# Two unused strips in SBUF that move every operand of the two MLPs

## Chip, cores and metric

The kernel runs on one core of a Trainium2 chip. The metric is the device time of one execution in microseconds (us). Before the change it is 952.58 us, the median of three runs (951.78 to 953.23).

## What is computed

The reference is a linear attention over 4 x 8 heads of 576 x 64, whose output, laid out as 2304 tokens of 512 features, goes through two MLPs one after the other:

```
phi(x): proj = x @ w_phi; proj -= max|proj|; concat(exp(proj), exp(-proj))
attn = (phi(q) @ (phi(k)^T v)) / (phi(q) . sum(phi(k)) + 1e-6)
MLP 1: h = x @ w_in;  g = h if h > 0 else exp(min(h, 0)) - 1;   x = g @ w_out
MLP 2: h = x @ w_in;  g = h * clip(h + 3, 0, 6) / 6;            y = g @ w_out
```

Both MLPs have 512 features and 2048 hidden units. Their weights arrive as 64-bit floats and are turned into 32-bit floats on the chip.

## The kernel before

**Order of work.** A planner (`in_order`) gives every step an engine, a length and a rank and writes out one order for all engines; TensorE's order in the MLPs is written by hand (the list `order`). Attention takes the first 158 us or so, in eight units; the rest is the MLPs.

**How an MLP is tiled.** The tokens are cut into four blocks of 512 and one of 256 (`BLOCKS`). The hidden units are walked in 8 groups g of 256 per MLP (g = 0 to 7 is MLP 1, g = 8 to 15 is MLP 2). For the blocks in pairs (pr = 0 and pr = 1) the first product is made in Strassen's way, from seven products P1 to P7 whose token operands are the tiles A11, A12, A22, S1, S2, S3 and S4 of that pair; the last block goes the plain way (`hid4`). The tables that say which operand a product uses are:

```
TERMS = {
    "P1": ("A11", "B11"), "P2": ("A12", "B21"), "P3": ("S4", "B22"), "P4": ("A22", "T4"),
    "P5": ("S1", "T1"), "P6": ("S2", "T2"), "P7": ("S3", "T3"),
}
```

**The matmuls.** Every 32-bit operand is kept as a high and a low part in the type fp32r, and a product is three matmuls: high x high, high x low, low x high. There are three kinds of matmul group:
- P groups (`hid`, L710): six matmuls of 512 columns; the weights `w_in` are stationary, the token tile `x_...` moves. 14 in each g.
- H groups (`hid4`, L724): twelve matmuls of 256 columns with the token tile `x_b4`. 2 in each g.
- O groups (`outp`, L775): six matmuls. In MLP 1 the stationary operand is `w_out` and the gated tile `ga` or `gb` moves, 512 columns for 16 groups of each g and 256 columns for 4; in MLP 2 `ga`/`gb` is stationary and `w_out` moves, always 512 columns, 18 groups in each g.

In a middle g the order is: H, O, H, O O O, P1 P2 of pair 0, O O, P6, O O, P5 P7, P1 of pair 1, P3 of pair 0, O, P4 of pair 0, O, P2 of pair 1, O O, P6, O O, P5 P7, O, P3, O, P4, O O (from P2 on all of pair 1; the two O after P3 and P4 of pair 0 are the last block's). The profile drops buffer numbers: `x_A` is any of A11, A12, A22 and `x_S` any of S1 to S4, so this order says which one a row is.

**What is done around them.** ScalarE and VectorE gate a finished P or H group in PSUM (L744 to L758: the last two write the high and low parts of `ga`/`gb`), VectorE adds finished O groups to the sum in `x32` (L787), ScalarE, VectorE and GpSimd convert and split weights (L626 to L677). A P or H group needs a free PSUM bank, which the low part (L758) of an earlier group frees. Between the MLPs, at g = 8, the token operands are made anew from the finished sums (`prepare`, L687 to L696).

**Where the tiles lie.** SBUF is filled from both ends of each partition, and each tile begins on a multiple of 32 bytes. From the left: 1,152 bytes of scratch and constants, then `x32` at 1,152, `ident` at 38,016, `half_c` and `two_c`, and the unused tile `gap` (496 bytes) at 38,592. After it come the pools `wp` (`w_in`, `w_out`), `stg` (the conversion), `early` (five operands of pair 0: A11, A12, A22, S1, S3) and `att_b`, later `mlp_b` (all seven operands of pair 1). `wp` begins at 39,104 = 76 x 512 + 192, all its tiles and those of the other MLP pools are whole multiples of 512 bytes long, and the slices that TensorE reads begin at multiples of 512 within a tile: so these operands all begin at remainder 192, counted modulo 512. From the right: the pools of attention and later `mlp_a` (S2 and S4 of pair 0, `x_b4`, `ma`, `mb`, `ga`, `gb`), which ends at 229,344 = 447 x 512 + 480: these all begin at remainder 480.

Of the kernel before, what the change touches and what calls it, by code (L numbers as in the profile page):

```python
# [8 lines left out]
F32 = mybir.dt.float32  # L9
# [139 lines left out]
def attention_then_two_mlps(  # L149
# [49 lines left out]
    const = ctx.enter_context(tc.tile_pool(name="const", bufs=1))  # L199
# [17 lines left out]
    nc.gpsimd.memset(half_c, 0.5)  # L217
    two_c = const.tile([128, 1], F32, name="two_c")
    nc.gpsimd.memset(two_c, 2.0)
    const.tile([128, 124], F32, name="gap")  # L220

    wp = ctx.enter_context(tc.tile_pool(name="wp", bufs=1))
    stg = ctx.enter_context(tc.tile_pool(name="stg", bufs=1))
# [928 lines left out]
```

## Time and profile before

| | |
|---|---|
| median of three runs | 952.58 us |
| the profiled execution | 952.91 us |
| its span, first to last instruction | 950.8 us |
| TensorE matmul busy | 918.8 us (97% of the span) |
| TensorE weight load busy | 762.3 us (80%) |
| VectorE, ScalarE, GpSimd busy | 676.0, 566.6, 399.7 us |
| mean granted TensorE clock | 0.990 |

Busy times of TensorE are of pipelined instructions: each matmul of 512 columns is shown some 390 to 397 ns long, and the next one starts long before it ends. The pace is therefore read from the starts: in a timeline of TensorE alone, a row is a run of equal matmuls, and the start of the next row less its own start, over its count, is the time of one. Its starts are rounded to 0.01 us.

### The profile page before, as it was taken

The page shows a single profiled execution, that of the slowest core. Times are in us where ns is not written, and L with a number is a line of the kernel's source. Part 1 is how long each engine was busy: PE and PEld are TensorE (multiplying, and loading weights), DVE is VectorE, ACT ScalarE, POOL GpSimd, SP SyncE. Part 2 cuts the span into 40 slices and gives each one's busy share as a digit, 9 for nine tenths or more (in the row PEclk, how much of TensorE's full clock was granted, in tenths as well). Part 3 has the DMA queues.
Part 4 walks back from the last instruction along what each step waited for, and adds up shares of the span by engine and source line. Part 5 has one row for each costly group of instructions (what it writes and reads, how often), then busy time and mean ns, then how long its engine had stood idle before and what let it go on. Part 6 is the DMA issues. An engine that isn't in the chain of part 4 may idle for free.

```text
span 950.8 us, 17635 instructions
## 1 busy us (share of the span) xinstructions
PE 918.8 (97%) x6792; PEld 762.3 (80%) x6792; DVE 676.0 (71%) x1202; ACT 566.6 (60%) x1207; POOL 399.7 (42%) x570
## 2 busy tenths in 40 slices
PE   8999999899999999999999968999999999999998
PEld 7888787688888888888878856888888888888886
DVE  6888877855676767676767797467767676777555
ACT  5686766876665656565666755665545454545331
POOL 0258621453544444444442646545444444444200
PEclk9999999999999999999999987999999999999999
DMA  8534510001111111111111001111111111010013
GB/s 228 160 110 124 147 47 2 1 27 41 45 45 45 45 46 45 45 44 46 45 42 43 29 22 36 43 56 55 46 56 34 57 34 56 33 56 23 1 67 133
DMA packets 42532, 53.69 MB, mean 56 GB/s; under 512 B 21328, under 2 KB 21456, under 8 KB 42448
## 3 DMA queue, kind: packets, MB, share of 16 engines
q1 hardware_dynamic: 42448, 52.57, 17.8%
q8 instruction: 53, 0.87, 0.4%
q14 instruction: 31, 0.25, 0.1%
HBM read 47.84 MB, written 4.72 MB: 55 GB/s over the span
## 4 chain that ended last, share of the span: by engine, by line
PE 88%; DVE 6%; ACT 5%; issue 1%; POOL 0%; POOLq 0%; ACTq 0%
PE ps_a L775 27%; PE ps_p L710 25%; PE ps_t L775 13%; PE ps_t L710 6%; PE ps_t L430 4%; PE ps_a L380 4%; PE ps_p L724 3%; PE ps_p L318 3%; ACT e L407 2%; DVE x L687 1%; DVE x_S L696 1%; PE ps_t L452 1%; PE ps_t L724 1%; DVE x L787 1%; DVE x_A L696 1%
## 5 line engine op out<-in xcount | busy, mean ns | idle before, releaser
L710 PE MATMUL ps_p<-x_S,w_in 128*128 128x512 f32 x630 | 162.6, 397 | 10.0 <-POOL x_S L696 4.1
L787 DVE TENSOR_TENSOR x<-ps_a,x 128x512 f32<-128x512 f32 (+1 forms) x177 | 116.4, 660 | 50.4 <-PE ps_a L775 49.0
L710 PEld LDWEIGHTS ps_p<-x_S,w_in 128*128 128x128 f32 x630 | 118.4, 189 | 39.4 <-POOL x_S L696 4.9
L710 PE MATMUL ps_p<-x_A,w_in 128*128 128x512 f32 x468 | 120.9, 399 | 3.4 <-DVE ga L758 3.4
L668 POOL TENSOR_TENSOR w_in<-w_bi,w_in 128x256 fp32r<-128x256 f32 x128 | 97.7, 782 | 44.7 <-ACT w_in L664 44.2
L635 POOL TENSOR_SCALAR w_a<-w_a 128x256 f32<-128x256 f32 x128 | 53.9, 422 | 146.5 <-ACT w_a L630 146.1
L710 PEld LDWEIGHTS ps_p<-x_A,w_in 128*128 128x128 f32 x468 | 88.5, 191 | 23.3 <-DVE ga L758 4.2
L787 DVE TENSOR_TENSOR x<-ps_t,x 128x512 f32<-128x512 f32 (+1 forms) x89 | 59.0, 663 | 43.0 <-PE ps_t L775 42.6
L651 POOL TENSOR_TENSOR w_bi<-w_bi,w_a 128x256 int32<-128x256 int32 x64 | 47.9, 757 | 95.0 <-DVE w_a L647 95.0
L677 POOL TENSOR_TENSOR w_out<-w_bo,w_out 128x256 fp32r<-128x256 f32 x64 | 48.1, 751 | 94.3 <-ACT w_out L673 93.6
L775 PE MATMUL ps_a<-w_out,gb 128*128 128x512 f32 x336 | 84.9, 395 | 0.0
L775 PE MATMUL ps_a<-gb,w_out 128*128 128x512 f32 (+1 forms) x384 | 83.2, 358 | 0.6 <-DVE x L787 0.6
L651 POOL TENSOR_TENSOR w_bo<-w_bo,w_a 128x256 int32<-128x256 int32 x64 | 48.3, 756 | 65.0 <-DVE w_a L647 62.3
L775 PEld LDWEIGHTS ps_a<-gb,w_out 128*128 128x128 f32 x384 | 64.8, 188 | 13.2 <-DVE x L787 0.8
L775 PEld LDWEIGHTS ps_a<-w_out,gb 128*128 128x128 f32 x336 | 63.0, 188 | 15.1 <-ACT x L785 0.2
L751 DVE SCALAR_TENSOR_TENSOR ps_p<-ma,ps_p 128x512 f32<-128x512 f32 x66 | 45.8, 693 | 30.8 <-ACT ma L747 16.4
L775 PE MATMUL ps_a<-ga,w_out 128*128 128x512 f32 x258 | 65.6, 395 | 0.5 <-DVE ga L758 0.5
L732 ACT COPY mb<-ps_p 128x512 f32<-128x512 f32 x54 | 31.7, 587 | 57.1 <-PE ps_p L710 56.9
L328 DVE TENSOR_REDUCE mx<-ps_p 128x4 f32<-128x512 f32 (+1 forms) x80 | 50.3, 629 | 15.7 <-PE ps_p L318 15.4
L775 PE MATMUL ps_a<-w_out,ga 128*128 128x512 f32 x240 | 60.1, 397 | 0.0
L775 PEld LDWEIGHTS ps_a<-ga,w_out 128*128 128x128 f32 x258 | 47.6, 188 | 11.6 <-DVE ga L758 0.9
L630 ACT ACTIVATE w_a<-w 128x256 f32<-128x256 f32 x128 | 54.3, 424 | 1.1 <-POOL w_bo L651 1.1
(109 smaller groups left out, 1907.1 us busy)
## 6 DMA issues: line engine op xcount, KB each, us to landing
w<-in_moe_w_in_dram SPq DMA_DIRECT2D x64, 256.0 KB, 2.6
w<-in_moe_w_out_dram SPq DMA_DIRECT2D x64, 256.0 KB, 2.6
vb<-in_v_dram SPq DMA_DIRECT2D x16, 288.0 KB, 4.2
out_dram<-x SPq DMA_DIRECT2D x18, 256.0 KB, 2.0
raw_k<-in_k_dram SPq DMA_DIRECT2D x7, 576.0 KB, 4.5
raw_q<-in_q_dram SPq DMA_DIRECT2D x7, 576.0 KB, 4.9
raw_k<-in_k_dram SPq DMA_DIRECT2D x1, 320.0 KB, 4.9
raw_q<-in_q_dram SPq DMA_DIRECT2D x1, 320.0 KB, 5.3
```

What stands on the lines that cost most here:

```text
L328: V.tensor_reduce(out=mx[:, :n], in_=P[j, h], axis=AX.X, op=ALU.max, apply_absolute_value=True)
L380: nc.tensor.matmul(out=acc[bb][f0:f0 + 64, h, half], lhsT=kp[p, i, half, f0:f0 + 64], rhs=vb[u % 2][p, r, h], start=(done.count(bb) == 1 a ...
L430: nc.tensor.matmul(out=ps[p, i, h], lhsT=E[h, c][:, half, r - 4 * c, p], rhs=ST[0][:, bb, h, half], start=(half == 0), stop=(half == 1),)
L630: nc.scalar.activation(out=st["a"], in_=s.bitcast(F32).rearrange("p (n t) -> p n t", t=2)[:, :, 1], func=AF.Abs)
L635: nc.gpsimd.tensor_scalar(out=st["a"], in0=st["a"], scalar1=W_MOST, scalar2=W_LEAST, op0=ALU.min, op1=ALU.max)
L651: nc.gpsimd.tensor_tensor(out=b_, in0=b_, in1=st["a"].bitcast(I32), op=ALU.add)
L668: nc.gpsimd.tensor_tensor(out=t[:, 1], in0=F[key], in1=t[:, 0].bitcast(F32), op=ALU.subtract)
L677: nc.gpsimd.tensor_tensor(out=t[:, 1], in0=F.pop((m, w, 1, c)), in1=t[:, 0].bitcast(F32), op=ALU.subtract)
L710: nc.tensor.matmul(out=PS[ps_], lhsT=t[:, a_, kk], rhs=X[pr, op][x_][kk], start=(opens and i == 0), stop=(i == 5), skip_group_check=True,)
L751: V.scalar_tensor_tensor(out=PS[ps_], in0=MAIN[key], scalar=s, in1=PS[ps_], op0=o0, op1=o1)
L775: nc.tensor.matmul(out=o, lhsT=a_, rhs=b_, start=(fi + j == 0), stop=(fi == 1 and j == 2))
L787: V.tensor_tensor(out=part, in0=ps, in1=part, op=ALU.add)
```

## The change

The unused tile `gap` grows from 124 to 208 floats, and a second unused tile of 120 floats is taken from the right end before any other pool of that side is opened. Nothing else is edited; no instruction is added, removed or reordered.

```diff
-    const.tile([128, 124], F32, name="gap")
+    const.tile([128, 208], F32, name="gap")
+    ctx.enter_context(tc.tile_pool(name="gap", bufs=1, side="right")).tile([128, 120], F32, name="gap_r")
```

On the left everything behind `gap` moves up by 320 bytes: `wp` begins at 39,424 = 77 x 512. On the right everything moves down by 480 bytes: `mlp_a` ends at 228,864 = 447 x 512. So every TensorE operand of the MLPs begins at remainder 0. `x32` and `ident` stay at remainder 128.

## Rows read from the trace of the kernel before

**Rows 1.** The page: busy time, share of the span and instructions of each engine.
```profile
PE 918.8 (97%) x6792; PEld 762.3 (80%) x6792; DVE 676.0 (71%) x1202; ACT 566.6 (60%) x1207; POOL 399.7 (42%) x570
```

**Rows 2.** Windows of all engines: a stretch's length, busy times, clock.
```profile
core 0: us, PE busy (x) PEld busy (x) DVE busy (x) ACT busy (x) POOL busy (x), PEclk, DMA share, GB/s
...
158.00:200.00 42.00, 38.41 (x261) 30.21 (x260) 31.58 (x46) 32.02 (x65) 17.18 (x13) 1.00 0.00 1
...
560.00:600.00 40.00, 32.53 (x125) 25.88 (x124) 28.25 (x40) 22.31 (x45) 24.21 (x25) 0.82 0.13 40
...
744.00:792.00 48.00, 48.00 (x221) 39.50 (x220) 34.32 (x60) 25.07 (x55) 21.87 (x34) 1.00 0.15 45
```

**Rows 3.** Timeline of TensorE, MLP 1: start, length of the run, count.
```profile
start us, us, engine line op out<-in xcount [idle before <-releaser]
...
269.22 1.56 PE L775 MATMUL ps_a<-gb,w_out 128*128 128x512 f32 x6
270.62 1.55 PE L710 MATMUL ps_t<-x_S,w_in 128*128 128x512 f32 x6
272.01 1.52 PE L710 MATMUL ps_p<-x_S,w_in 128*128 128x512 f32 x6
273.37 1.52 PE L710 MATMUL ps_p<-x_A,w_in 128*128 128x512 f32 x6
274.73 1.56 PE L710 MATMUL ps_t<-x_S,w_in 128*128 128x512 f32 x6
276.13 0.87 PE L775 MATMUL ps_a<-gb,w_out 128*128 128x256 f32 x6
276.83 0.86 PE L775 MATMUL ps_t<-gb,w_out 128*128 128x256 f32 x6
```

**Rows 4.** The same timeline, the last block and one g's first groups.
```profile
260.88 1.55 PE L710 MATMUL ps_t<-x_A,w_in 128*128 128x512 f32 x6
...
298.45 1.56 PE L775 MATMUL ps_a<-gb,w_out 128*128 128x512 f32 x6
299.99 1.67 PE L724 MATMUL ps_p<-x_b,w_in 128*128 128x256 f32 x12
301.50 1.56 PE L775 MATMUL ps_a<-ga,w_out 128*128 128x512 f32 x6
302.90 1.56 PE L724 MATMUL ps_p<-x_b,w_in 128*128 128x256 f32 x12
304.30 1.56 PE L775 MATMUL ps_t<-ga,w_out 128*128 128x512 f32 x6
...
308.49 1.55 PE L710 MATMUL ps_p<-x_A,w_in 128*128 128x512 f32 x6
```

**Rows 5.** Timeline of TensorE in MLP 2, one g.
```profile
660.70 2.91 PE L710 MATMUL ps_p<-x_A,w_in 128*128 128x512 f32 x12
...
673.18 1.52 PE L710 MATMUL ps_t<-x_A,w_in 128*128 128x512 f32 x6
674.54 1.56 PE L710 MATMUL ps_p<-x_S,w_in 128*128 128x512 f32 x6
...
681.49 2.96 PE L775 MATMUL ps_a<-w_out,ga 128*128 128x512 f32 x12
684.29 1.53 PE L710 MATMUL ps_t<-x_S,w_in 128*128 128x512 f32 x6
...
707.92 2.91 PE L710 MATMUL ps_p<-x_A,w_in 128*128 128x512 f32 x12
```

**Rows 6.** Timeline of TensorE where MLP 1 ends and MLP 2 begins.
```profile
570.51 2.76 PE L710 MATMUL ps_t<-x_A,w_in 128*128 128x512 f32 x6
573.07 2.13 PE L724 MATMUL ps_p<-x_b,w_in 128*128 128x256 f32 x12
```

**Rows 7.** Timeline of VectorE ahead of the H group at 299.99.
```profile
298.65 0.69 DVE L787 TENSOR_TENSOR x<-ps_t,x 128x512 f32<-128x512 f32 x1 [0.70 <-PE ps_t L775]
299.25 0.68 DVE L758 TENSOR_TENSOR ga<-ps_p,ga 128x512 fp32r<-128x512 f32 x1
```

## The prediction

> **What bounds the kernel now.** I read the page's busy times first, then the windows, then the timeline of TensorE alone. TensorE is busy for 97% of the span [rows 1], and in the middle of an MLP for all of it: 48.00 of 48.00 us, VectorE 34.32, ScalarE 25.07, GpSimd 21.87, DMA 0.15 [rows 2]. Busy time of pipelined matmuls proves little, so the timeline is the main view: there one run of matmuls follows the next with no idle time between them but at the start of a g [rows 3 to 5], and a whole g repeats, from its first P group to that of the next: 308.49 - 260.88 = 47.61 us in MLP 1, 707.92 - 660.70 = 47.22 us in MLP 2 [rows 4, 5]. So in the MLPs the time is the number of matmuls times their pace, and every nanosecond of the pace counts some 3,500 times (by the order 228 matmuls in a g of MLP 1, 216 in one of MLP 2, eight g each). Only three places are bounded otherwise: attention, the first g (38.41 busy of 42.00 us), and the change of MLPs, where TensorE is busy for 32.53 of 40.00 us at a mean granted clock of 0.82 [rows 2].
>
> **The pace is not the same everywhere.** This is what the reader should see in [rows 3]. The P group at 272.01 and the one at 273.37 take 1.36 us each for six matmuls: 226.7 ns, or 544 cycles at 2.4 GHz for 512 columns. The P group right behind them, at 274.73, takes 1.40 us: 233.3 ns, or 560 cycles. All three are the same line, shape and kind of weights, at the full clock and with no wait. By the order of the groups they are P7 of pair 0 (S3), P1 of pair 1 (A11) and P3 of pair 0 (S4). S3 and A11 lie on the left, at remainder 192 as `w_in` does; S4 of pair 0 lies on the right, at remainder 480. MLP 2 repeats it: A11 of pair 1 takes 674.54 - 673.18 = 1.36 us, and the O groups at 681.49 take 2.80 us for twelve, 1.40 for six [rows 5]. There `ga` (480) is stationary and `w_out` (192) moves; in MLP 1 it is the other way round, and the O groups at 269.22 and 298.45 take 1.40 too [rows 3, 4]. So 544 cycles go with two operands at the same remainder, whichever kind of group it is, 560 with two that differ, and it does not matter which of the two is at 480. The groups of 256 columns all pair 480 with 192: the H group at 302.90 takes 1.40 us for twelve, 116.7 ns or 280 cycles each, and the O group at 276.13 0.70 us for six [rows 3, 4]. 560 is 512 x 35/32 and 280 is 256 x 35/32: a share, not a fixed cost. A P group between O groups pays part of it: S1 at 270.62, both operands at 192, takes 1.39 us behind an O group, and 1.36 is reached by the group after it [rows 3]: the faster rhythm has to be found again.
>
> I read this as a conflict of two read streams: while one operand moves, the weights of the next matmul are loaded from the same memory, and they get in each other's way less when they begin at the same place modulo 512. The kernel now pairs like with like only in the P groups that don't take S2 or S4 of pair 0.
>
> **The change part by part.** It adds no instruction, wait or transfer. It moves all these operands to remainder 0, so that all pairs are like with like.
>
> *512 columns and 256 columns.* I take 1.36 us for six of 512 and 12 x 113.3 ns = 1.36 us for twelve of 256; the latter is an estimate, the same 34/32 as at 512 columns, since no row shows 256 columns with like remainders. Its bounds are 1.36 and the present 1.40. One g of MLP 1 is 14 P, 16 O and 2 H groups and four O groups of half length: 32 x 1.36 + 4 x 0.68 = 46.24 us. To this comes the pause ahead of the first H group: the O group at 298.45 should give way at 299.85, H begins at 299.99 and takes 1.51 where 1.40 is usual [rows 4], so 0.14 + 0.11 = 0.25 us. It will grow. The H group waits for a PSUM bank that `ga`'s low part (299.25 + 0.68 = 299.93) frees; VectorE comes to that only after a sum at 298.65, which waits for the O group before [rows 7]. That chain keeps its length of 1.3 us while the O group running beside it shrinks from 1.40 to 1.36: 0.04 us more. So 46.24 + 0.29 = 46.53, against 47.61: 1.08 us less in each g. There are six such g, g = 1 to 6: 6.5 us. The last g of MLP 1 (g = 7) also has the eight O groups of its second half moved in from behind, and the first two P groups of MLP 2 follow it without a break: by the list `order` 16 P, 24 O and 2 H groups, 42 equal lengths at 1.08 / 34 = 0.032 us each: 1.3 us.
>
> One g of MLP 2 is 14 P, 18 O and 2 H groups: 34 x 1.36 = 46.24 us, against 47.22: 0.98 us less. From 600 us, where the window with the lowered clock ends [rows 2], to the end of the span at 950.8 are 351 us, less a few for the last sum and store: 7.35 g, 7.2 us.
>
> *First g and the change of MLPs.* Much of both is waiting for other engines. Of the first g I count a fifth of a g's gain, 0.2 us; of the change of MLPs nothing. There the bounds are wide on both sides. At the half clock a group takes 573.07 - 570.51 = 2.56 us [rows 6] against 1.40; two or three groups more or less in such a stretch are 3 us, and the stretches hang on when the waits fall, which the change shifts. I take 0 and keep +-3.
>
> *Coming back to the fast rhythm.* Behind a pause the first group may take 1.39, as behind an O group today: 0.03 us. With the pause in each g of MLP 1 and the waits between the MLPs I count ten places: 0.3 us back.
>
> *Other engines.* VectorE's L787, whose SBUF operand is `x32` at 128, takes 0.69 us, and L758, whose SBUF operand is at 480, 0.68 [rows 7]: its pace does not follow the remainder, and the engines have slack if it did a little. VectorE's 34.32 us in 48 [rows 2] become 34.3 in 47: the cover stays. Attention has mostly pairs from the same side, which move together; I count 0, with +-0.3.
>
> Sum: 6.5 + 1.3 + 7.2 + 0.2 - 0.3 = 14.9 us. The profiled execution took 952.91 us (span 950.8, 2.1 around it, which stay), 0.33 above the median of the runs, so 938.0 by it and **937.7 us** by the median. If the 256-column groups keep 1.40, MLP 1 loses 4 of its 34 equal lengths and MLP 2 2 of its 34: (8 x 4 + 8 x 2) x 0.04 = 1.9 us, 939.6. With the change of MLPs the likeliest case reaches from 934 to 941.
>
> **The rivals.**
> *No effect.* The operands are moved, and the pace does not follow: 952.6 us. The right strip might not hold, so that the right side stays at 480 and all unlike pairs stay unlike (480 against 0), which gives the same time. Against it: the strip is taken in the way `gap` is. The Trainium skill has a rule by which the address would not matter: the page "TensorE: Matmul & The Clock Gate", section "Step-by-step: what each phase is for", says that the moving operand and the weight load have independent read ports and that loading the next weights takes no read bandwidth from the running matmul. By that rule the sum would be 0; by [rows 3] it is 14.9 us, and the step from 1.36 to 1.40 with nothing but the tile changed speaks for the rows. What keeps the rival alive is that tiles on the right differ from those on the left in more than the remainder. 5%.
>
> *Half of it is taken back.* TensorE gets its pace, but waits appear: P2 of pair 1 and the H groups wait for banks that chains over ScalarE and VectorE free, and these don't get faster. For it: the pause at every H group of MLP 1 shows that one such chain has no slack [rows 4, 7]. Against it: the chain begins with a TensorE group itself, so it shifts along, and MLP 2 shows no pause. If each g of both MLPs paid 0.5 us, 16 x 0.5 = 8 us go: 945 us. 10%.
>
> *Slower: the place itself counts, not the likeness.* The runs at 1.36 us have both operands at 192; none is at 0. If two streams that both start at remainder 0 meet head on, the 1.36 groups fall to 1.40 and the others stay: of 14 P groups per g 12 are like with like today, at 1.36 to 1.39, so some 0.025 us each, 16 x 12 x 0.025 = 4.8 us: 957 us. It decides from the first P groups of MLP 1 on: a P group behind a P group at 1.40. Against it: a conflict that goes by the difference of two addresses does not know where they lie. 5%.
>
> **How the numbers follow.** The likeliest case, 80%, gives 937.7 us with its own range 934 to 941; the case of half 945, 10%; no effect 952.6, 5%; slower 957, 5%. The range for 8 in 10 reaches from 934 to 945: what is left out are the last two cases and the tails. About 0.2% (1.9 us) is what a measurement of this kernel can tell from no change. Faster by more than that: 0.90; within it: 0.05; slower: 0.05.
>
> **What would show it.** In the timeline of TensorE after the change: O groups of 512 columns at 1.36 us and S4 of pair 0 at the pace of S3 beside it; H groups at 1.36 for twelve; one g at 46.5 us in MLP 1 and 46.2 in MLP 2; the pause at the H group 0.2 to 0.3 us and no new one. The prediction is wrong if O groups stay at 1.40, if a g shortens by less than 0.7 us, or if the change of MLPs moves by more than 3 us.

## The result, and the profile after

The changed kernel takes 941.05 us, the median of four runs (940.39 to 941.19), against 952.9 us before, the median of four runs as well (the three known earlier and one more): a ratio of 0.9876 with a 95% interval of 0.9859 to 0.9893. The forecast was 937.7 us in a range of 934 to 945. The sign, the place and the pace of the groups of 512 columns are as forecast; the gain is 11.9 us instead of 14.9 us by the sum.

The profiled execution took 940.39 us, its span 938.3. The page of the changed kernel, busy times (compare [rows 1]): every engine runs as many instructions as before, TensorE's busy time is 14 us shorter, and that of each other engine moves by less than 2 us.

```profile
PE 904.8 (96%) x6792; PEld 762.1 (81%) x6792; DVE 674.2 (72%) x1202; ACT 566.1 (60%) x1207; POOL 400.6 (43%) x570
```

The timeline of TensorE in MLP 1 after the change, the stretch that answers to [rows 3] and [rows 4] (the edit adds one line, so L710 is L711 here, and so on):

```profile
start us, us, engine line op out<-in xcount [idle before <-releaser]
...
260.28 1.52 PE L711 MATMUL ps_t<-x_A,w_in 128*128 128x512 f32 x6
...
268.44 1.52 PE L776 MATMUL ps_a<-gb,w_out 128*128 128x512 f32 x6
269.80 1.52 PE L711 MATMUL ps_t<-x_S,w_in 128*128 128x512 f32 x6
271.16 1.52 PE L711 MATMUL ps_p<-x_S,w_in 128*128 128x512 f32 x6
272.52 1.52 PE L711 MATMUL ps_p<-x_A,w_in 128*128 128x512 f32 x6
273.88 1.52 PE L711 MATMUL ps_t<-x_S,w_in 128*128 128x512 f32 x6
275.24 0.88 PE L776 MATMUL ps_a<-gb,w_out 128*128 128x256 f32 x6
275.95 0.88 PE L776 MATMUL ps_t<-gb,w_out 128*128 128x256 f32 x6
...
297.20 1.52 PE L776 MATMUL ps_a<-gb,w_out 128*128 128x512 f32 x6
298.75 1.69 PE L725 MATMUL ps_p<-x_b,w_in 128*128 128x256 f32 x12
300.27 1.55 PE L776 MATMUL ps_a<-ga,w_out 128*128 128x512 f32 x6
301.66 1.59 PE L725 MATMUL ps_p<-x_b,w_in 128*128 128x256 f32 x12
303.10 1.55 PE L776 MATMUL ps_t<-ga,w_out 128*128 128x512 f32 x6
...
307.20 1.52 PE L711 MATMUL ps_p<-x_A,w_in 128*128 128x512 f32 x6
```

Read the differences of the starts. The O group at 268.44, S1 behind it and S4 of pair 0 at 273.88 now all take 1.36 us; before they took 1.40, 1.39 and 1.40. The groups of 256 columns went the other way: the H group at 301.66 takes 1.44 us for twelve where it took 1.40, the half O group at 275.24 0.71 instead of 0.70. And the group of 512 columns behind each of them starts out of step: 1.39 us at 300.27 and 1.38 at 303.10. A whole g takes 307.20 - 260.28 = 46.92 us instead of 47.61. Over g = 1 to 6, 983 of the 1,104 matmuls of 512 columns now start 226 or 227 ns before the next one; before the change 178 did.

MLP 2 after the change (compare [rows 5]): A11 of pair 1 and S4 of pair 0 both take 1.36 us, the twelve O matmuls at 673.53 take 2.72 us instead of 2.80, and a g 699.57 - 653.13 = 46.44 us instead of 47.22.

```profile
653.13 2.88 PE L711 MATMUL ps_p<-x_A,w_in 128*128 128x512 f32 x12
...
665.37 1.52 PE L711 MATMUL ps_t<-x_A,w_in 128*128 128x512 f32 x6
666.73 1.52 PE L711 MATMUL ps_p<-x_S,w_in 128*128 128x512 f32 x6
668.09 1.52 PE L776 MATMUL ps_a<-w_out,gb 128*128 128x512 f32 x6
...
673.53 2.88 PE L776 MATMUL ps_a<-w_out,ga 128*128 128x512 f32 x12
676.25 1.52 PE L711 MATMUL ps_t<-x_S,w_in 128*128 128x512 f32 x6
...
699.57 2.88 PE L711 MATMUL ps_p<-x_A,w_in 128*128 128x512 f32 x12
```

Where the time went, by the starts of the same matmuls in both profiled executions. The 3,552 matmuls of the MLPs are counted from 0, and the stages are cut at numbers 0, 228, 1596, 1823, 2040 and 3551. The first column names the g that lies between two cuts; number 1823 is the last one before the waits at the change of MLPs.

| stage | before, us | after, us | saved | forecast |
|---|---|---|---|---|
| up to the first MLP matmul | 157.89 | 158.22 | -0.3 | 0 +- 0.3 |
| g = 0 | 55.13 | 54.94 | 0.2 | 0.2 |
| g = 1 to 6 | 288.73 | 284.27 | 4.5 | 6.5 |
| g = 7 | 48.73 | 47.75 | 1.0 | 1.3, with the next two P groups |
| g = 8, the change of MLPs | 62.99 | 61.51 | 1.5 | 0 +- 3 |
| g = 9 to 15 | 333.11 | 327.37 | 5.7 | 7.2, with the end of g = 8 |

### The profile page after: what moved, and what is told of

Read it like the earlier page. It is cut to its first block, busy times and chain, and to the rows that moved or that the text cites. A ratio compares the mean times of both kernels' runs of the same rounds, so it can differ in the third digit from the quotient of the medians.

```text
span 938.3 us, 17635 instructions
## 1 busy us (share of the span) xinstructions
PE 904.8 (96%) x6792; PEld 762.1 (81%) x6792; DVE 674.2 (72%) x1202; ACT 566.1 (60%) x1207; POOL 400.6 (43%) x570
## 4 chain that ended last, share of the span: by engine, by line
PE 88%; DVE 6%; ACT 5%; issue 1%; DMA 0%; POOL 0%; POOLq 0%; ACTq 0%; SPq 0%
PE ps_a L776 27%; PE ps_p L711 25%; PE ps_t L776 13%; PE ps_t L711 6%; PE ps_a L381 4%; PE ps_t L431 4%; PE ps_p L725 3%; PE ps_p L319 3%; ACT e L408 2%; DVE x L688 1%; DVE x_S L697 1%; PE ps_t L453 1%; PE ps_t L725 1%; DVE x_A L697 1%; DVE x L788 1%
## 5 line engine op out<-in xcount | busy, mean ns | idle before, releaser
L711 PE MATMUL ps_p<-x_S,w_in 128*128 128x512 f32 x630 | 160.1, 393 | 10.6 <-POOL x_S L697 4.6
L711 PEld LDWEIGHTS ps_p<-x_S,w_in 128*128 128x128 f32 x630 | 118.1, 189 | 37.6 <-POOL x_S L697 5.4
L711 PE MATMUL ps_p<-x_A,w_in 128*128 128x512 f32 x468 | 120.0, 397 | 3.7 <-DVE ga L759 3.7
L711 PEld LDWEIGHTS ps_p<-x_A,w_in 128*128 128x128 f32 x468 | 88.5, 191 | 22.5 <-DVE ga L759 4.5
L776 PE MATMUL ps_a<-w_out,gb 128*128 128x512 f32 x336 | 82.8, 389 | 0.0
L776 PEld LDWEIGHTS ps_a<-w_out,gb 128*128 128x128 f32 x336 | 63.0, 188 | 13.3 <-ACT x L786 0.2
```

The source lines that it names most:

```text
L711: nc.tensor.matmul(out=PS[ps_], lhsT=t[:, a_, kk], rhs=X[pr, op][x_][kk], start=(opens and i == 0), stop=(i == 5), skip_group_check=True,)
L776: nc.tensor.matmul(out=o, lhsT=a_, rhs=b_, start=(fi + j == 0), stop=(fi == 1 and j == 2))
```

## The experiments

The theory after the result: the pace of a matmul goes by the distance, modulo some power of two, between where the moving operand begins and where the weights that are loaded meanwhile begin. What was still open: whether the multiple of 512 matters or only the likeness, which modulus it is, whether the moving operand meets its own weights or the next ones, and why 256 columns got slower. The edits below are against the changed kernel, and `...` marks lines left out.

**The left strip alone.**

```diff
     const.tile([128, 208], F32, name="gap")
-    ctx.enter_context(tc.tile_pool(name="gap", bufs=1, side="right")).tile([128, 120], F32, name="gap_r")
```

> The left strip alone: the left pools at remainder 0, the right ones still at 480. Theory (likeness of the two remainders sets the pace): every pair that was like stays like, every unlike pair stays unlike (480 against 0), so O groups of 512 columns at 1.40 us for six, P groups of two left operands at 1.36 behind another P group, groups of 256 columns at 1.40 for twelve, 47.6 us for one g of MLP 1, 952 to 953 us in all. Rival (each operand that comes to remainder 0 gains for itself): w_in, w_out and most token tiles are now at 0, so some of the gain appears, 945 to 948 us. A third (the difference in bytes matters, not only like or unlike): the difference is now 32 bytes, it was 288, and O groups take another pace than 1.40.

Measured: 953.01 us, ratio to before 1.000 (0.999 to 1.0011). The timeline of TensorE in this kernel, the same stretch as above:

```profile
269.77 1.56 PE L775 MATMUL ps_a<-gb,w_out 128*128 128x512 f32 x6
271.17 1.55 PE L710 MATMUL ps_t<-x_S,w_in 128*128 128x512 f32 x6
272.55 1.52 PE L710 MATMUL ps_p<-x_S,w_in 128*128 128x512 f32 x6
273.91 1.52 PE L710 MATMUL ps_p<-x_A,w_in 128*128 128x512 f32 x6
275.27 1.56 PE L710 MATMUL ps_t<-x_S,w_in 128*128 128x512 f32 x6
276.67 0.51 PE L775 MATMUL ps_a<-gb,w_out 128*128 128x256 f32 x3
```

The O group at 269.77 takes 1.40 us, S3 and A11 1.36, S4 of pair 0 1.40: as before, though the weights and all left token tiles are now at multiples of 512. An aligned operand gains nothing for itself; the rival falls. The third text, that the difference in bytes matters, gets no support from the O groups, which keep 1.40; but the second H group of this g takes 1.42 us for twelve (304.87 - 303.45) where 1.40 was expected, so the difference does matter a little at 256 columns. For 512 columns this run could hardly tell. With the modulus of 256 bytes that is found below, the two distances that an unlike pair can have, moving operand less weights and the other way round, are 32 and 224 bytes both before and here, only exchanged; and the bursts below give 560 cycles for 512 columns at both.

**Both sides at 192.**

```diff
-    const.tile([128, 208], F32, name="gap")
-    ctx.enter_context(tc.tile_pool(name="gap", bufs=1, side="right")).tile([128, 120], F32, name="gap_r")
+    const.tile([128, 124], F32, name="gap")
+    ctx.enter_context(tc.tile_pool(name="gap", bufs=1, side="right")).tile([128, 72], F32, name="gap_r")
```

> The left side as before the change, at remainder 192, and a right strip of 72 floats that brings the right side to 192 too. No operand lies at a multiple of 512. Theory (likeness): as the changed kernel, O groups 1.36 us, groups of 256 columns 1.43 for twelve, 940 to 942 us. Rival (the multiple of 512 counts): O groups stay at 1.40 or find another pace, 947 to 953 us.

Measured: 942.26 us, ratio to before 0.9891 (0.9874 to 0.9907), where the change has 0.9876 (0.9859 to 0.9893). The timeline of TensorE in this kernel:

```profile
268.68 1.52 PE L776 MATMUL ps_a<-gb,w_out 128*128 128x512 f32 x6
270.04 1.52 PE L711 MATMUL ps_t<-x_S,w_in 128*128 128x512 f32 x6
271.40 1.52 PE L711 MATMUL ps_p<-x_S,w_in 128*128 128x512 f32 x6
272.76 1.52 PE L711 MATMUL ps_p<-x_A,w_in 128*128 128x512 f32 x6
274.12 1.52 PE L711 MATMUL ps_t<-x_S,w_in 128*128 128x512 f32 x6
275.48 0.88 PE L776 MATMUL ps_a<-gb,w_out 128*128 128x256 f32 x6
```

Every group of 512 columns in these rows takes 1.36 us with no operand at a multiple of 512. By the stages of the table above, g = 1 to 6 take 284.39 us here and 284.27 in the change, g = 9 to 15 327.37 in both. So likeness gives the gain, and no effect of the place shows. The median is 0.3 us above the expected 940 to 942; the groups at the change of MLPs (g = 8) took 62.63 us here and 61.51 in the profile of the change.

**The law of the pace, in bursts.** Behind the changed kernel's own work, with everything else idle:

```diff
...
+    for off in (0, 32, 64, 96, 128, 192, 256, 320, 384, 480):
+        for n in (512, 384, 256, 128):
+            for i in range(24):
+                o = off // 4 + 512 * (i % 2)
+                nc.tensor.matmul(
+                    out=px[:, :n], lhsT=wl[:, 128 * (i % 4):128 * (i % 4) + 128], rhs=RAW[1, "A11"][:, o:o + n],
+                    start=True, stop=True,
+                )
```

> The changed kernel with forty bursts of 24 matmuls behind the MLPs, whose results nobody reads: the moving operand starts 0, 32, 64, 96, 128, 192, 256, 320, 384 and 480 bytes off a multiple of 512, the stationary ones at multiples of 512; 512, 384, 256 and 128 columns at each. What a matmul costs with like remainders: if a fixed 32 cycles at 2.4 GHz come on top, as 544 for 512 and 288 for 256 columns suggest, 384 columns take 416 cycles (173.3 ns) and a burst of 24 4.16 us; 512 5.44 us, 256 2.88 us, 128 1.60 us unless the weight load bounds it. If it were a share of 1/16, 384 columns take 408 cycles and 4.08 us. With unlike remainders: a share of 3/32, so 512 columns 560 cycles and 5.60 us, 256 columns 280 cycles and 2.80 us, 384 columns 420 cycles and 4.20 us, the same at every offset but 0 if 512 is the modulus; if it is smaller (256, 128, 64), 256, 128 or 64 bytes off behave as 0.

Measured, from the starts of the single matmuls in the second half of each burst, in cycles at 2.4 GHz, good to about one cycle (the granted clock is 1.00 throughout):

| bytes off | 0, 256 | 32 | 64, 320 | 96 | 128, 384 | 192 | 480 |
|---|---|---|---|---|---|---|---|
| 512 columns | 544 | 560 | 549, 550 | 561 | 561, 559 | 561 | 560 |
| 384 columns | 416 | 424 | 416 | 424 | 422 | 419 | 416 |
| 256 columns | 288 | 283 | 283 | 289 | 285 | **272** | 283 |
| 128 columns | 268 | 268 | 267 | 268 | 268, 267 | 268 | 268 |

The entries at 256, 320 and 384 bytes repeat those at 0, 64 and 128 (480 has no such partner here), and 128 bytes differ from 0: the modulus is 256 bytes, not 512 and not less. With like remainders the cost on top of the columns is a fixed 32 cycles, as 512, 384 and 256 columns show (544, 416, 288), not the share of 1/16 that the prediction took over from 512 columns. And the idea that all unlike distances cost the same 3/32 fell as well: 64 bytes off is nearly as good as like at 512 columns, and at 256 columns a distance of 192 is the best of all, with 272 cycles. At 128 columns the distance makes no difference: 268 cycles. What bounds these was not looked into.

**The modulus in the kernel itself.**

```diff
-    ctx.enter_context(tc.tile_pool(name="gap", bufs=1, side="right")).tile([128, 120], F32, name="gap_r")
+    ctx.enter_context(tc.tile_pool(name="gap", bufs=1, side="right")).tile([128, 56], F32, name="gap_r")
```

> The right strip of 56 floats instead of 120: the right side at remainder 256, the left at 0, unlike modulo 512, like modulo 256. Theory (modulus 256, as in the bursts): as the changed kernel, O groups at 1.36 us, groups of 256 columns at 1.43 for twelve, 940 to 942.5 us. Rival (modulus 512): O groups at 1.40, 950 to 953 us.

Measured in one run: 941.27 us. Its TensorE timeline has S4 of pair 0, on the right side, at 274.77 - 273.41 = 1.36 us, as S3 and A11 ahead of it:

```profile
270.69 1.52 PE L711 MATMUL ps_p<-x_S,w_in 128*128 128x512 f32 x6
272.05 1.52 PE L711 MATMUL ps_p<-x_A,w_in 128*128 128x512 f32 x6
273.41 1.52 PE L711 MATMUL ps_t<-x_S,w_in 128*128 128x512 f32 x6
274.77 0.88 PE L776 MATMUL ps_a<-gb,w_out 128*128 128x256 f32 x6
```

**Whose weights?** Fifteen bursts of 48 matmuls (`N_` is 48), each on its own line. In the fourth and fifth, shown here, the remainders alternate (the moving operand's stand first): in the fourth a matmul's own pair is alike and the next weights unlike, in the fifth the other way round.

```diff
...
+    def mm(n, i, mov, sta):
+        o, w = mov // 4 + 512 * (i % 2), sta // 4 + 128 * (i % 2)
+        return dict(out=px[:, :n], lhsT=wl[:, w:w + 128], rhs=xl[:, o:o + n], start=True, stop=True)
...
+    for i in range(N_):
+        nc.tensor.matmul(**mm(512, i, (0, 96)[i % 2], (0, 96)[i % 2]))
+    for i in range(N_):
+        nc.tensor.matmul(**mm(512, i, (0, 96)[i % 2], (96, 0)[i % 2]))
```

> The changed kernel with fifteen bursts of 48 matmuls behind the MLPs, each on a line of its own, whose results nobody reads. Fourth and fifth burst (512 columns): moving and stationary operands alternate between 0 and 96 bytes off. In the fourth each matmul's own two operands are alike and the next one's weights are unlike what moves; in the fifth it is the other way round. Theory (what moves conflicts with the load of the next weights): the fourth runs at the unlike pace, about 560 cycles or 11.2 us for 48, the fifth at 544 cycles, 10.9 us. Rival (a matmul's own two operands count): the fourth 10.9, the fifth 11.2 us. The others repeat the earlier bursts at twice the length, so that the way into the rhythm weighs less: 512 columns at 0 and 256 off 10.9 us, at 96, 128 and 192 off 11.2, at 64 off 11.0; 384 columns at 0 off 8.32 us (a fixed 32 cycles; 8.16 if a share of 1/16), at 96 off 8.49; 256 columns at 0 off 5.76 us, at 32 off 5.66, at 192 off 5.44; 128 columns 5.3.

The timeline of TensorE over some of the bursts; a row's start to that of the next is its 48 matmuls:

```profile
936.19 11.22 PE L1108 MATMUL ps_law<-x_A,w_in 128*128 128x512 f32 x48 [0.78 <-DVE x L789]
947.24 11.37 PE L1110 MATMUL ps_law<-x_A,w_in 128*128 128x512 f32 x48
...
969.68 11.39 PE L1114 MATMUL ps_law<-x_A,w_in 128*128 128x512 f32 x48
980.91 11.20 PE L1116 MATMUL ps_law<-x_A,w_in 128*128 128x512 f32 x48
991.95 11.17 PE L1118 MATMUL ps_law<-x_A,w_in 128*128 128x512 f32 x48
...
1025.30 11.08 PE L1124 MATMUL ps_law<-x_A,w_in 128*128 128x512 f32 x48
1036.22 8.51 PE L1126 MATMUL ps_law<-x_A,w_in 128*128 128x384 f32 x48
1044.57 8.64 PE L1128 MATMUL ps_law<-x_A,w_in 128*128 128x384 f32 x48
```

The burst whose own pairs are alike (969.68) takes 11.23 us, 234.0 ns per matmul, as slow as the wholly unlike one (947.24: 11.21). So a matmul's own two operands are not what counts, and that rival falls. The burst with like next weights (980.91) takes 11.04 us, 230.0 ns or 552 cycles: faster, but not the 544 that was expected; the steps between its starts alternate between 224 and 236 ns. (The first burst, alike throughout, takes 11.05 us as a whole, because it begins behind a pause: its first step is 341 ns, and in its second half it is at 544 cycles.) The fourth and the fifth burst move the same operands in the same order and differ only in whether the weights are alike with their own matmul or with the one ahead of it, so the weights that come next do count. That nothing else counts is not borne out: here the moving operand also jumps by 96 bytes from one matmul to the next. What that jump does stays open, and so does what the two streams share: no run leaves the weight loads out. The burst 256 bytes off (1025.30) takes 10.92 us, the like pace; 384 columns with like remainders (1036.22) take 8.35 us, near the 8.32 of a fixed cost and not the 8.16 of a share. The bursts of 256 columns repeat the table: 5.75 us at 0 bytes off, 5.66 at 32 and 5.45 at 192.

**Groups of 256 columns at the better distance.** First the token tile of the H groups, then also, in MLP 1, the gated tile of the last block:

```diff
-        t = pools["a"].tile([128, 2, KD, 256], F32R, name="x_b4")
+        t = pools["a"].tile([128, 2 * KD * 256 + 64], F32R, name="x_b4")
+        t = t[:, 48:48 + 2 * KD * 256].rearrange("p (a k n) -> p a k n", a=2, k=KD)
```

```diff
-        GG[key] = pools["a"].tile([128, 2, 512], F32R, tag=ring, name=ring, bufs=rings[ring])
+        t = pools["a"].tile([128, 1024 + 64 * (ring == "gb")], F32R, tag=ring, name=ring, bufs=rings[ring])
+        o = 48 if key[1] == 4 and key[0] < NP else 0
+        GG[key] = t[:, o:o + 1024].rearrange("p (a n) -> p a n", a=2)
```

> The changed kernel once more, to stand beside the next two on one chip: 940 to 942.5 us.

> The changed kernel with the token tile x_b4 moved by 192 bytes within its place, so that the moving operand of the H groups (256 columns) starts 192 bytes off the weights, modulo 256. Theory (modulus 256; 256 columns cost 288 cycles at like remainders and 272 at 192 bytes off, as in the bursts): H groups at 1.36 us for twelve instead of 1.43, 32 of them, 2.2 us less than the changed kernel: 938 to 939.5 us. Rival (the burst's 272 cycles hold only in a long run of equal matmuls, and a group of twelve between groups of other widths never reaches them): H groups stay at 1.40 to 1.43, no change of time.

> The same, and in MLP 1 also the gated tile of the last block moved by 192 bytes, so that all groups of 256 columns pair that way. Theory: the 32 half O groups at 0.68 us for six instead of 0.71 to 0.72, 1.1 us less again: 937 to 938.5 us, which is what was predicted for the change with 113.3 ns per matmul of 256 columns. Rival as before: no change.

Measured on one chip: the change 941.63 us, ratio to before 0.988 (0.9866 to 0.9895); with the H groups moved 939.63, 0.9858 (0.9842 to 0.9875); with both moved 939.93, 0.9865 (0.985 to 0.988). The intervals overlap, so the times alone don't settle it. The profiles do, by the stages of the table above: g = 1 to 6 take 284.29 us in the change, 283.85 with H moved, 283.29 with both; g = 7 47.75, 47.66 and 47.64; g = 9 to 15 327.37, 326.81 and 326.81. That is 1.1 us for the first step and 0.6 for the second, where 2.2 and 1.1 were expected. The timeline of TensorE with the H groups moved shows why only half came:

```profile
298.70 1.64 PE L726 MATMUL ps_p<-x_b,w_in 128*128 128x256 f32 x12
300.18 1.54 PE L777 MATMUL ps_a<-ga,w_out 128*128 128x512 f32 x6
301.56 1.58 PE L726 MATMUL ps_p<-x_b,w_in 128*128 128x256 f32 x12
302.97 1.52 PE L777 MATMUL ps_t<-ga,w_out 128*128 128x512 f32 x6
304.33 2.88 PE L777 MATMUL ps_a<-ga,w_out 128*128 128x512 f32 x12
```

The H group at 301.56 takes 1.41 us, where the change had 1.44, and the O group behind it 1.36 instead of 1.38. The starts within the two H groups tell theory and rival apart: the first, which begins behind its pause, reaches 113.3 ns (272 cycles) from its seventh matmul on; the second, which follows the 512-column rhythm without a pause, stays at 117.7 ns (282 cycles) through all twelve. The other g's agree in the main: all 14 H groups of MLP 2 from 597 us on, where no pause comes before them, stay at 117.7 ns in both kernels (1.41 us). Behind the pause of a middle g of MLP 1, three of five reach 113.3 ns with the H groups moved, and five of five with both moved. So at this distance 256 columns have more than one rhythm, and how they are entered has a part in which one they fall into; a pause alone does not decide it. Both texts were half right. Both kernels have the lower medians, 1.7 to 2.0 us below the change, about the 0.2% that a measurement can tell.

## Why the prediction was right, and which term was mis-sized

**The bound and the pace by likeness: right.** The groups of 512 columns came to 1.36 us, S4 of pair 0 and the O groups of both MLPs among them; only those right behind a group of 256 columns take 1.38 to 1.39. No new wait took the place of the gain. Two things need putting right. The remainders count modulo 256 bytes and not 512; the change could not show that, because remainder 0 is alike in both. And that the conflict is one of reading the same memory is not shown: the runs show that the start of the next weights counts (561 against 552 cycles in the alternating bursts), not what the two streams share.

One of the prediction's own signs of being wrong came close. A g was to shorten by 0.7 us at least; the g's from 2 to 5 shortened by about 0.70 to 0.72 (the one shown by 0.69 by its rounded rows) and those of MLP 2 by 0.78, where 1.08 and 0.98 were forecast. The next paragraph says where the rest went.

**The term that was mis-sized: 256 columns.** The prediction took the H groups at 1.36 us for twelve, as "an estimate, the same 34/32 as at 512 columns", and bounded it by the 1.40 of before. They take 1.43 to 1.44, outside these bounds, and 1.52 behind the pause of a g of MLP 1: the cost is a fixed 32 cycles, which is twice as large a share of 256 columns as of 512. In the g of MLP 1 shown above that is 0.05 us more than forecast at the H group behind the pause, 0.08 at the other and 0.16 at the four half O groups; the 512-column group behind each of four such places is out of step by 0.02 to 0.03, 0.09 in all, and the pause is 0.01 longer: 46.53 + 0.39 = the 46.92 measured. In MLP 2 it is two H groups and two such places: 46.24 + 0.20 = 46.44. Over the g's that the sum counted this is some 2.7 and 1.5 us, 4.2 of the forecast 14.9. The profiled execution saved 12.5 us all the same, and in part by luck: 1.5 of it came from the change of MLPs, which was counted as nothing. The two lengths seen with unlike remainders, 560 and 280 cycles, suggested a share, and the bursts at 384 columns do not keep it: 424 and 416 cycles at 32 and 480 bytes off, where a share of 3/32 makes 420. The error was to carry a share over to like remainders, where only one length had been seen; a fixed cost fitted that one point as well, and the upper bound should have allowed for it: (288 - 280) / 2.4 = 3.3 ns per matmul above the present.

**The pause at the H groups: right.** The O group at 297.20 would give way at 298.56; H begins at 298.75, a pause of 0.19 us where 0.14 + 0.04 was forecast.

**Coming back to the fast rhythm** was sized at ten places and 0.3 us. It happens at every change from 256 to 512 columns too: there the first five steps or so are between 228 and 236 ns before 226 to 227 is reached. Why is not shown; in the kernel with the H groups moved it is there behind H groups at 113.3 ns and missing behind most of those at 117.7.

**The change of MLPs** gave 1.5 us in this profile, within the +-3. It is not a property of the change: g = 8 took 62.99 us before, 61.51 after, and in the second profile of the same changed kernel 62.87. What differs is where the half clock falls. The windows below are those of before, of the changed kernel and of its second profile (columns as in [rows 2]). Ahead of 560 us the granted clock is 0.94 before, 1.00 after and 0.86 in the second profile; behind it, it is 0.82, 0.83 and 0.91:

```profile
535.00:560.00 25.00, 21.54 (x102) 17.37 (x101) 23.07 (x40) 16.81 (x35) 15.03 (x16) 0.94 0.07 22
...
535.00:560.00 25.00, 18.76 (x95) 15.10 (x93) 24.66 (x42) 16.72 (x35) 14.45 (x13) 1.00 0.04 11
560.00:600.00 40.00, 34.35 (x139) 27.88 (x140) 28.58 (x42) 24.00 (x50) 27.95 (x32) 0.83 0.11 34
...
535.00:560.00 25.00, 21.29 (x96) 17.19 (x95) 23.21 (x38) 14.31 (x29) 12.91 (x12) 0.86 0.03 11
560.00:600.00 40.00, 31.26 (x130) 24.96 (x129) 29.71 (x44) 25.49 (x54) 27.02 (x30) 0.91 0.11 34
```

Of the eight profiles of kernels without bursts, two have a g = 8 of 61.5 us, this one and that of the kernel with both moved, and in both the clock ahead of 560 us is 1.00; the others have 62.6 to 63.2. That the clock makes the difference fits this, but no run isolates it. Without this stage the profiled execution, the fastest of the four runs, saved about 11 us.

**The rivals.** *No effect* and *slower by the place* are refuted, the second by the P groups that keep 1.36 us at remainder 0; the kernel with both sides at 192 is as fast. That tiles on the right differ from those on the left in more than the remainder, which kept *no effect* alive, falls with the kernels in which the right strip alone is changed: S4 of pair 0 takes 1.40 us without that strip and 1.36 with the one that brings it to remainder 256. *Half taken back by waits* did not come: what was lost was lost in the pace. The rule quoted with the first rival, from the Trainium skill's page "TensorE: Matmul & The Clock Gate", section "Step-by-step: what each phase is for", that loading the next weights takes no read bandwidth from the running matmul, is not enough to give the time of these matmuls: with the other engines idle, 512 columns take 544 to 561 cycles by where the two streams begin, and 561 or 552 by which weights come next. Whether it is read bandwidth that is lost, no run here shows. The Trainium skill's page "TensorE: Matmul & The Clock Gate", section "Wait — 56ns, not 53.3ns?", gives a warm matmul N / 2.4 GHz plus about 2.5 ns. Here the best pace of 512 columns, 226.7 ns, has 13.3 ns on top, and that of 256 columns, 113.3 ns, has 6.7.

## What to carry to other kernels

Where TensorE is the bound and every matmul loads new weights, read the pace from the starts, by kind of operand: if the same shape runs at two paces, look at where the two operands begin. For these fp32r matmuls of 512 columns (and, by the bursts alone, of 384) the moving operand and the weights should begin at the same remainder modulo 256 bytes; a pad of a few hundred bytes between pools did that here and gave 1.2%. For matmuls of 256 columns the best distance in a long burst was another one, and only half of what it promised came in the kernel: measure in the order in which the matmuls run, not in a long burst of equals. At 128 columns the distance made no difference.

## What the runs showed of the hardware

- The pace of back-to-back fp32r matmuls that each load new weights repeats with the distance of the two operands every 256 bytes, as far as tried: 544 cycles for 512 columns at 0 and 256, 549 to 550 at 64 and 320, 559 to 561 at 32, 96, 128, 192, 384 and 480.
- At 256 columns the like distance is among the slow ones (288 cycles), and 192 bytes the fastest (272) in a long run.
- The rhythm has a memory: behind a pause or a change of length or distance it takes some five to eleven matmuls of 512 columns to settle (five behind groups of 256 columns in the changed kernel, about eleven in the first and the ninth burst of 48). Groups of 256 columns at 192 bytes settle at 272 or 282 cycles, at 282 in all 14 groups of MLP 2 that follow 512 columns without a pause.
- At 128 columns a matmul with new weights takes 267 to 268 cycles (111.7 ns at 268) at every distance tried, little less than one of 256 columns.
